# Casting reloaded weights some units after their load, and moving four small loads to another queue

## The chip, the cores and the metric

The kernel runs on one core of a Trainium2 chip. The metric is the device time of one execution in microseconds (us), from runs of the same program with the same inputs. The core has a matrix engine (PE, whose weight loads PEld are listed apart), a vector engine (DVE), a scalar engine (ACT), a third elementwise engine (POOL) and a synchronisation engine (SP) that here only issues DMA transfers. Each engine works through its own instructions in a fixed order and waits on semaphores for the results of the others. An engine that issues DMAs does so in that same order, so a waiting instruction also holds back the DMAs behind it.

## The reference

An attention with random features is followed by a gated MLP:

```python
def phi(x):                                   # x: q or k, scaled by D**-0.25
    proj = einsum('bhsd,md->bhsm', x, omega)
    h = proj - sum(x * x, -1, keepdims=True) / 2
    return exp(h - max(h, -1, keepdims=True)) / sqrt(m)
kv  = einsum('bhsm,bhsd->bhmd', k_p, v);  z = sum(k_p, 2)
out = einsum('bhsm,bhmd->bhsd', q_p, kv) / (einsum('bhsm,bhm->bhs', q_p, z) + 1e-6)

x = out.transpose(0, 2, 1, 3).reshape(4608, 512)
g = x @ w_gate;  y = (g / (1 + exp(-g)) * (x @ w_val)) @ w_out
```

Batch and heads are 8 and 8, the sequence is 576, the head size 64, and there are 128 random features. The MLP has 4608 tokens, a model width of 512 and an inner width of 1536. All inputs are 32-bit floats.

## The kernel before

**Attention** goes in steps. A step n holds one group of k and one of q of two heads, and is cut into pieces: `st_transpose` (PE, and the copy `x` on ACT at L408), `st_project` (PE `pp`, L423), `st_max` (DVE, L437 to L447), `st_exp` (ACT `ph`, L459, eight exponentials), `k_accumulate` (PE `kvacc`, L561, with v as its other operand), `q_transpose` (PE `ptq`, ACT `qt`), `q_mult` (PE `po`, L602), `q_norm` (DVE `xn`, L612) and `q_out` (PE `xt`, ACT `xo` L657, a store to DRAM). When a head's k groups are all in, `kvacc` is copied by ACT (`kvr`, L475), and PE transposes its last column (`zp`, L481). `kvacc` has a single PSUM buffer. A sequence of 576 is one group of 512 rows and a rest of 64; the rest's v is the tile `vrest`, loaded at L365, the other v tiles at L358.

**The MLP** runs between the attention's pieces, as soon as tokens are there. A 32-bit product is made of three passes of PE over a high part and a low part of each operand: `whi*xh`, `whi*xl`, `wlo*xh` (`mm1`, L678, for gate g and value v; `mm2`, L687, for the output product o). It goes by nine tiles of 512 tokens. The inner width is cut into 12 blocks, three to a weight set, so four sets. Tiles 0 to 4 visit the four sets in 20 visits; at six places the next visit needs another set, and the new weights take the place of the old in SBUF. Tiles 5 to 8 are done in pairs at the end by a scheme of seven products (L912). A visit is a sequence of units that a generator `stream()` yields: three g units, three v units, four o units, each 12 or 9 matmuls. `give()` draws units from it between the attention's pieces, so a unit is the clock of the MLP.

**Weights.** `convert_all` reads the raw weights once (the tile `st`), rounds them on ACT (L277, L289), DVE (L280 to L286) and POOL (L291) into a tile `wc`, and stores that to a DRAM scratch `wscr` (L295). When a set is changed, `load_weights` fetches a block back from the scratch (`wraw`, L323), and `split_piece` makes the two parts: ACT casts `whi` (L251) and POOL subtracts `wlo` (L252). `wc` and `wraw` share three buffers under the tag `wraw`, so a fetch waits until an earlier tile has been split, and a conversion waits for the same buffers. Reloads of gate blocks (i = 0) are asked for behind the silu of the last visit with the old set, those of value blocks (i = 1) behind each v unit, and those of output blocks (i = 2) behind the last o unit: nine blocks at each of six changes, 54 in all.

**Order.** A scheduler decides at build time, from simulated times and the order of the code, in which order each engine executes. `behind_step()` tells it that an instruction stands behind the step's last exponential on ACT and the last biased operation on DVE (`step_end`); the conversion uses it, `load_weights` does not. The k and q loads (`nat`) have three buffers and are asked for three steps ahead, as are those of v.

Of the kernel before, what the change touches and what calls it, by code (L numbers as in the profile page):

```python
# [23 lines left out]
def kernel(  # L24
# [11 lines left out]
    nc = tc.nc  # L36
# [86 lines left out]
    AHEAD = 6  # L123
# [69 lines left out]
    for n in range(NN + 1):  # L193
        vi = 0
# [111 lines left out]
    def need(f, i):  # L306
        while (f, i) not in converted:
            tick()

    def load_weights(f, i):  # L310
        need(f, i)
        fetched = fetch((f,), i)
        new_weights(f, i)
        split_piece(f, i, fetched[0])

    def fetch(fs, i, spare=None):
        raws_ = []
# [60 lines left out]
    def load_v(n):  # L378
        for i, b, g, gr in slots(n, "k"):
            rest = gr is None  # L380
            ts = (vtile, vrest)[rest]
            t = ts[nv[rest] % len(ts)]
            nv[rest] += 1
            assert t not in busy, "v's tile is still needed"
            busy.append(t)
            vrows[b, g] = t
            load_group(t, v, b, gr, True, nc.scalar if n == 0 or n < AHEAD and gr is None else nc.sync)

    box = {}
    sts = {}  # L390
# [314 lines left out]
    def down(j, k_, ht, wts, next_set, tt):  # L705
        fs = sorted(ht)
        po = ps_moe(f"o{j}_{k_}_{tt}", [P, DM])
        for n, f in enumerate(fs):
            need(f, 2)
            mm2(po, ht[f], weights[f, 2] if wts is None else wts[f], tt, n == 0, n == len(fs) - 1)  # L710
        if k_ == 0:
            acc[j, tt] = accp.tile([P, DM], F32, name=f"acc{j}_{tt}", tag="acc")
            nc.scalar.copy(acc[j, tt], po)
        else:
            a_ = acc[j, tt]
            nc.vector.tensor_tensor(a_, po, a_, op=ALU.add)  # L716
        if k_ == (NPF if j in paired else NSET) - 1:
            a_ = acc.pop((j, tt))
            for o in range(0, P, RES):
                nc.sync.dma_start(rows_of(TILES[j][0] + tt * P + o), a_[o : o + RES, :])  # L720
        if next_set is not None and tt == TILES[j][1] // P - 1:
            for f in next_set:
                load_weights(f, 2)

    def stream():

        todo = []
        for vi, (j, s_, k_) in enumerate(visits):
# [14 lines left out]
            pg, ht = {}, {}  # L743
            for f in fs:
                need(f, 0)
                pg[f] = ps_moe(f"g{vi}_{f}", [P, T])[:, 0:w]
                mm1(pg[f], weights[f, 0], xs)
                yield mm1_us(w)
# [15 lines left out]
                fetch_x(nxt[0])  # L764
            for f in fs:
                need(f, 1)
                pv = ps_moe(f"v{vi}_{f}", [P, T])[:, 0:w]
                mm1(pv, weights[f, 1], xs)
                yield mm1_us(w)
                h = pg[f]  # L770
                nc.vector.tensor_tensor(h, pv, h, op=ALU.mult)  # L771
                hh = moe.tile([P, T], F32R, name=f"hh{vi}_{f}", tag="hh", bufs=FA)[:, 0:w]
                hl = moe.tile([P, T], F32R, name=f"hl{vi}_{f}", tag="hl", bufs=FA)[:, 0:w]
                nc.scalar.copy(hh, h)  # L774
                nc.gpsimd.tensor_tensor(hl, h, hh.bitcast(F32), op=ALU.subtract)  # L775
                ht[f] = hh, hl
                if new_set:
                    load_weights(nxt[1] * FA + f - fs[0], 1)
            if final:
                make_seven((0, 0), 1, fetch((0, 1), 1))  # L780
            wts = {f: weights[f, 2] for f in fs} if vi else None
            then = range(nxt[1] * FA, nxt[1] * FA + FA) if new_set else None
            todo = [(j, k_, ht, wts, then, tt) for tt in range(w // P)]
# [267 lines left out]
    def give(us):  # L1051
        debt[0] += us
        while debt[0] > 0:
            u = next(ma, None)
            if u is None:
                debt[0] = 0.0
                return False
            debt[0] -= u
            given[0] += u
        return True  # L1060
# [108 lines left out]
```

## Time and profile before

| what | value |
|---|---|
| time, three runs | 1174.39, 1174.82, 1180.82 us; median 1174.82 us |
| the profiled execution's own time | 1172.79 us |
| its span, first to last instruction | 1171.0 us, 18724 instructions |
| PE busy | 1149.5 us (98%) |
| ACT, DVE, POOL busy | 678.3 us (58%), 630.0 us (54%), 569.1 us (49%) |
| granted PE clock | 0.999 |
| attention and MLP together, then the pairs | up to about 797 us, then to the end |

Busy time of an engine counts its instructions but not the issuing of DMAs. "ACTq" and "SPq" in a timeline are the DMA issues of ACT and SP: the duration is the time that the issue keeps the engine, not the transfer's. In a timeline a row is a run of equal instructions: start, duration of the whole run, engine, line, operation, `output<-inputs`, count, and in brackets the idle time before it with what ended it. The table of waits has, for each pair of waiting and awaited line, the total, the count and the longest. In the table of windows, each engine has its busy time and, in brackets, its number of instructions.

### The profile page before, as it was taken

To read this page: it belongs to the slowest core of one execution; us is meant where nothing else is said; L and a number is where in the kernel's file an instruction comes from. 1 tells how busy PE (TensorE), PEld (TensorE's weight loads), DVE (VectorE), ACT (ScalarE), POOL (GpSimd) and SP (SyncE) were. 2 spreads that over 40 slices of the span, in tenths; PEclk is the share of its full clock that TensorE was granted. 3 is DMA by queue.
4 is the path that set the end of the run, shared out by engine and by line. 5 is a ranking of instruction groups with operands and counts; after the bars stand their busy time and mean duration, and the time that the engine had idled before them with its cause. 6 is when DMAs were issued, how large, how long until landed. Compare 5 with 4: busy or idle time off the path is not lost.

```text
span 1171.0 us, 18724 instructions
## 1 busy us (share of the span) xinstructions
PE 1149.5 (98%) x6705; PEld 951.7 (81%) x6705; DVE 630.0 (54%) x1159; ACT 678.3 (58%) x1499; POOL 569.1 (49%) x500
## 2 busy tenths in 40 slices
PE   7999999999999999999999999999999999999998
PEld 6998778888888888888888777878778888888886
DVE  5876667535466554334332552462566666456654
ACT  5898887775666665665466665334544445444441
POOL 3342353433365465554445765244655543455551
PEclk9999999999999999999999999999999999999999
DMA  7654355643454442443232212424311112211103
GB/s 168 155 147 116 108 168 164 177 127 111 127 155 131 125 118 70 120 105 82 64 80 73 60 46 81 127 81 123 93 53 47 48 53 54 72 55 54 45 19 73
DMA packets 174109, 113.52 MB, mean 97 GB/s; under 512 B 125856, under 2 KB 144320, under 8 KB 174016
## 3 DMA queue, kind: packets, MB, share of 16 engines
q1 hardware_dynamic: 172096, 111.86, 35.2%
q8 instruction: 53, 0.87, 0.3%
q10 hardware_dynamic: 1920, 0.46, 0.2%
q14 instruction: 40, 0.33, 0.1%
HBM read 87.10 MB, written 25.18 MB: 96 GB/s over the span
## 4 chain that ended last, share of the span: by engine, by line
PE 73%; DVE 5%; ACT 3%; DMA 2%; issue 2%; POOL 1%; SPq 1%; POOLq 0%; DVEq 0%; ACTq 0%
PE o L687 22%; PE g L678 11%; PE a L912 10%; PE v L678 10%; PE c L912 5%; PE pp L423 3%; PE d L912 3%; PE kvacc L561 2%; PE ptq L585 2%; PE xt L642 2%; PE pt L400 1%; DMA wraw<-wscr 1%; ACT ph L459 1%; DMA first_b<-xs 1%; POOL wlo L252 1%
## 5 line engine op out<-in xcount | busy, mean ns | idle before, releaser
L407 POOL TENSOR_TENSOR sq<-nat 128x512 f32<-128x512 f32 x72 | 75.9, 1055 | 199.3 <-DVE st L437 157.3
L716 DVE TENSOR_TENSOR acc<-o,acc 128x512 f32<-128x512 f32 x140 | 95.6, 687 | 128.6 <-PE o L687 128.2
L459 ACT ACTIVATE ph<-pp,st 128x128 f32<-128x128 f32 x576 | 157.0, 387 | 6.4 <-DVE st L447 5.7
L444 DVE TENSOR_REDUCE st<-pp 128x4 f32<-128x512 f32 x144 | 93.3, 686 | 95.7 <-PE pp L423 95.4
L252 POOL TENSOR_TENSOR wlo<-wraw,whi 128x512 fp32r<-128x512 f32 x76 | 103.1, 1366 | 64.0 <-ACT whi L251 62.4
L678 PE MATMUL g<-xh,whi 128*128 128x512 f32 x240 | 96.3, 401 | 0.9 <-DVE sl L771 0.9
L678 PE MATMUL v<-xh,whi 128*128 128x512 f32 x240 | 95.6, 398 | 0.5 <-DVE acc L716 0.5
L687 PE MATMUL o<-whi,hh 128*128 128x512 f32 x240 | 95.9, 400 | 0.0
L423 PE MATMUL pp<-omT,x 64*128 64x128 f32 x1152 | 90.9, 289 | 4.6 <-ACT x L408 4.6
L687 PE MATMUL o<-whi,hl 128*128 128x512 f32 x240 | 93.8, 391 | 0.9 <-POOL hl L775 0.9
L775 POOL TENSOR_TENSOR hl<-sl,hh 128x512 fp32r<-128x512 f32 x60 | 77.9, 1302 | 33.7 <-ACT hh L774 33.5
L678 PE MATMUL g<-xl,whi 128*128 128x512 f32 x240 | 94.0, 392 | 0.0
L678 PE MATMUL g<-xh,wlo 128*128 128x512 f32 x240 | 94.0, 392 | 0.0
L678 PE MATMUL v<-xh,wlo 128*128 128x512 f32 x240 | 93.9, 391 | 0.0
L687 PE MATMUL o<-wlo,hh 128*128 128x512 f32 x240 | 93.9, 391 | 0.0
L678 PE MATMUL v<-xl,whi 128*128 128x512 f32 x240 | 93.6, 390 | 0.0
L423 PEld LDWEIGHTS pp<-omT,x 64*128 64x128 f32 x1152 | 73.9, 189 | 21.8 <-issue 11.6
L899 POOL TENSOR_TENSOR wlo<-wspare,whi 128x512 fp32r<-128x512 f32 (+1 forms) x40 | 40.5, 1032 | 75.0 <-ACT whi L898 68.6
L771 DVE TENSOR_TENSOR sl<-v,sl 128x512 f32<-128x512 f32 x60 | 40.9, 685 | 60.8 <-PE v L678 60.8
L251 ACT CAST whi<-wraw 128x512 fp32r<-128x512 f32 x76 | 46.6, 629 | 42.1 <-PE v L678 24.4
L525 DVE TENSOR_REDUCE dj<-jk 128x4 f32<-128x512 f32 x36 | 24.6, 685 | 83.8 <-POOL jk L521 69.1
L774 ACT CAST hh<-sl 128x512 fp32r<-128x512 f32 x60 | 37.5, 626 | 51.9 <-DVE sl L771 51.7
(257 smaller groups left out, 2938.4 us busy)
## 6 DMA issues: line engine op xcount, KB each, us to landing
wraw<-wscr SPq DMA_DIRECT2D x80, 256.0 KB, 2.7
wspare<-wscr SPq DMA_DIRECT2D x40, 256.0 KB, 2.7
wscr<-wc SPq DMA_DIRECT2D x36, 256.0 KB, 2.2
out_dram<-acc SPq DMA_DIRECT2D x72, 128.0 KB, 2.3
nat<-in_k_dram SPq DMA_DIRECT2D x64, 128.0 KB, 3.1
nat<-in_q_dram SPq DMA_DIRECT2D x64, 128.0 KB, 3.1
v<-in_v_dram SPq DMA_DIRECT2D x62, 128.0 KB, 3.0
st<-in_moe_w_gate_dram SPq DMA_DIRECT2D x12, 512.0 KB, 3.9
```

What stands on the lines that cost most here:

```text
L251: nc.scalar.copy(hi, raw)
L252: nc.gpsimd.tensor_tensor(lo, raw, hi.bitcast(F32), op=ALU.subtract)
L407: nc.gpsimd.tensor_tensor(sq, nat, nat, op=ALU.mult)
L423: nc.tensor.matmul(pp[hh][:, i, c, :], x[r, i, c * P : (c + 1) * P], omT[r], start=True, stop=True)
L444: nc.vector.tensor_reduce(st[:, 1, :, :, hh], pp[hh], axis=AX.X, op=ALU.max, negate=True)
L459: step_end["s"] = nc.scalar.activation(ph[:, c, hh * M : (hh + 1) * M], pp[hh][:, i, c, :], AF.Exp, bias=st[:, 3, i, c, hh : hh + 1], scal ...
L678: nc.tensor.matmul(ps, a_[:, ws], b_[:, c, :], start=n == 0, stop=n == 3 * NC - 1)
L687: nc.tensor.matmul(ps, a_[:, ts_], b_, start=first and n == 0, stop=last and n == 2)
L716: nc.vector.tensor_tensor(a_, po, a_, op=ALU.add)
L771: nc.vector.tensor_tensor(h, pv, h, op=ALU.mult)
L775: nc.gpsimd.tensor_tensor(hl, h, hh.bitcast(F32), op=ALU.subtract)
L912: nc.tensor.matmul(ps, a_[:, w_], b_[:, c, :], start=start and c == 0 and m == 0, stop=c == CH - 1 and m == 2, skip_group_check=True,)
```

## The change

`load_weights` now only asks for the fetch and puts the block in a list `landing` with a count of 3. `land()`, called after every unit that `give()` draws, counts all entries down; an entry at 0 gets its tiles and its cast and subtraction, now inside `behind_step()`. Where a weight is about to be used (`down`, the g and v units, and the choice of output weights of a visit), `land((f, i))` brings the list up to that block at once. So the cast stands three units behind the issue of the load, and behind the exponentials of the step. The conversion's own splits of the first set stay as they were. Second, the `vrest` loads of the first steps go to SP's queue; only step 0's are on ACT's.

```diff
--- before.py
+++ after.py
@@ -307,11 +307,22 @@
         while (f, i) not in converted:
             tick()
 
+    LAND = 3
+    landing = []
+
     def load_weights(f, i):
         need(f, i)
-        fetched = fetch((f,), i)
-        new_weights(f, i)
-        split_piece(f, i, fetched[0])
+        landing.append([LAND, f, i, fetch((f,), i)[0]])
+
+    def land(upto=None):
+
+        for t in landing:
+            t[0] -= upto is None
+        while landing and (landing[0][0] <= 0 or upto in [(f, i) for _, f, i, _ in landing]):
+            _, f, i, raw = landing.pop(0)
+            new_weights(f, i)
+            with behind_step():
+                split_piece(f, i, raw)
 
     def fetch(fs, i, spare=None):
         raws_ = []
@@ -384,7 +395,7 @@
             assert t not in busy, "v's tile is still needed"
             busy.append(t)
             vrows[b, g] = t
-            load_group(t, v, b, gr, True, nc.scalar if n == 0 or n < AHEAD and gr is None else nc.sync)
+            load_group(t, v, b, gr, True, nc.scalar if n == 0 else nc.sync)
 
     box = {}
     sts = {}
@@ -707,6 +718,7 @@
         po = ps_moe(f"o{j}_{k_}_{tt}", [P, DM])
         for n, f in enumerate(fs):
             need(f, 2)
+            land((f, 2))
             mm2(po, ht[f], weights[f, 2] if wts is None else wts[f], tt, n == 0, n == len(fs) - 1)
         if k_ == 0:
             acc[j, tt] = accp.tile([P, DM], F32, name=f"acc{j}_{tt}", tag="acc")
@@ -743,6 +755,7 @@
             pg, ht = {}, {}
             for f in fs:
                 need(f, 0)
+                land((f, 0))
                 pg[f] = ps_moe(f"g{vi}_{f}", [P, T])[:, 0:w]
                 mm1(pg[f], weights[f, 0], xs)
                 yield mm1_us(w)
@@ -764,6 +777,7 @@
                 fetch_x(nxt[0])
             for f in fs:
                 need(f, 1)
+                land((f, 1))
                 pv = ps_moe(f"v{vi}_{f}", [P, T])[:, 0:w]
                 mm1(pv, weights[f, 1], xs)
                 yield mm1_us(w)
@@ -778,6 +792,8 @@
                     load_weights(nxt[1] * FA + f - fs[0], 1)
             if final:
                 make_seven((0, 0), 1, fetch((0, 1), 1))
+            for f in fs if vi else ():
+                land((f, 2))
             wts = {f: weights[f, 2] for f in fs} if vi else None
             then = range(nxt[1] * FA, nxt[1] * FA + FA) if new_set else None
             todo = [(j, k_, ht, wts, then, tt) for tt in range(w // P)]
@@ -1055,6 +1071,7 @@
             if u is None:
                 debt[0] = 0.0
                 return False
+            land()
             debt[0] -= u
             given[0] += u
         return True
```

Behind the change the lines of the kernel are 11 to 14 higher: L365 is L376, L323 is L334, L408 is L419, L459 is L470, L475 is L486, L657 is L668, L752 is L765, L774 is L788, L775 is L789; L251 to L295 keep theirs.

The first place is the start of the program, on ACT and SP. ACT before (`om` is the matrix of random features, `x` the first scaled k and q):

```order
L334 DMA om_128<-in_omega_dram 128x64 x2
L358 DMA v_97<-in_v_dram 128x4x64
L358 DMA v_98<-in_v_dram 128x4x64
L365 DMA vrest_105<-in_v_dram 64x2x64 x4
L337 ACT_TABLE_LOAD
L337 ACTIVATE omT<-pt_om 128x128
L408 COPY x_150<-pt_145 128x512
```

and ACT in the changed kernel:

```order
L345 DMA om_128<-in_omega_dram 128x64 x2
L369 DMA v_97<-in_v_dram 128x4x64
L369 DMA v_98<-in_v_dram 128x4x64
L348 ACT_TABLE_LOAD
L348 ACTIVATE omT<-pt_om 128x128
L419 COPY x_150<-pt_145 128x512
```

The four `vrest` loads, which stood between the last v load and the load of the activation table, are gone from ACT. On SP at the same place, before (`nat` is k and q, the number behind a name tells tiles apart, `st_0` is a raw gate weight):

```order
L358 DMA v_100<-in_v_dram 128x4x64
L358 DMA v_101<-in_v_dram 128x4x64
L358 DMA v_102<-in_v_dram 128x4x64
L358 DMA v_103<-in_v_dram 128x4x64
L358 DMA nat_155<-in_k_dram 128x4x64 x2
L358 DMA v_104<-in_v_dram 128x4x64
L233 DMA st_0_343<-in_moe_w_gate_dram 128x4x256
L358 DMA nat_195<-in_k_dram 128x4x64 x2
L233 DMA st_0_459<-in_moe_w_gate_dram 128x4x256
L358 DMA nat_238<-in_k_dram 128x4x64 x2
```

and SP in the changed kernel:

```order
L369 DMA v_100<-in_v_dram 128x4x64
L376 DMA vrest_105<-in_v_dram 64x2x64 x4
L369 DMA nat_155<-in_k_dram 128x4x64 x2
L369 DMA v_101<-in_v_dram 128x4x64
L369 DMA v_102<-in_v_dram 128x4x64
L369 DMA v_103<-in_v_dram 128x4x64
L369 DMA nat_195<-in_k_dram 128x4x64 x2
L369 DMA v_104<-in_v_dram 128x4x64
L233 DMA st_0_343<-in_moe_w_gate_dram 128x4x256
L369 DMA nat_238<-in_k_dram 128x4x64 x2
```

The `vrest` loads now stand ahead of `nat_155`, the k of step 3 (counted from 0); `nat_195`, that of step 4, stands ahead of the raw weight `st_0_343` instead of behind it, `nat_238` behind it still, and the second raw weight, `st_0_459`, has gone further down.

The second place is ACT at the first change of set, from the last rows that the old set's visit has there to the copy of `kvacc` (`whi_0` and `whi_1` are casts of reloaded gate and value weights, `wc` and `st` belong to the conversion, `hh` and `sl` are the MLP's hidden values, the rest is the attention's). Before:

```order
L774 CAST hh_1_3078<-sl_1_2955 128x512
L251 CAST whi_1_3084<-wraw_1_3082 128x512
L289 ACTIVATE st_1_2903<-st_1_2903 128x512
L251 CAST whi_1_3121<-wraw_1_3119 128x512
L277 ACTIVATE wc_2_3140<-st_2_2990 128x512
L774 CAST hh_2_3115<-sl_2_2957 128x512
L752 ACT_TABLE_LOAD
L752 ACTIVATE sl_3_3253<-g_3_3125 128x512
L657 COPY xo_0_3_3150<-xt_0_3147 128x256
L587 COPY qt_2_3168<-ptq_2_3163 128x512
L475 COPY kvr_0_3174<-kvacc_0_2620 128x260
L408 COPY x_3207<-pt_3202 128x512
```

and in the changed kernel:

```order
L251 CAST whi_0_3085<-wraw_0_2961 128x512
L251 CAST whi_0_3089<-wraw_0_2963 128x512
L277 ACTIVATE wc_1_2980<-st_1_2903 128x512
L289 ACTIVATE st_1_2903<-st_1_2903 128x512
L788 CAST hh_2_3107<-sl_2_2957 128x512
L251 CAST whi_1_3126<-wraw_1_3043 128x512
L668 COPY xo_0_3_3142<-xt_0_3139 128x256
L765 ACT_TABLE_LOAD
L765 ACTIVATE sl_3_3253<-g_3_3113 128x512
L598 COPY qt_2_3160<-ptq_2_3155 128x512
L277 ACTIVATE wc_2_3132<-st_2_2978 128x512
L486 COPY kvr_0_3166<-kvacc_0_2620 128x260
```

The row ahead of this piece is the first `whi_0`, and ahead of that stands `hh_1`. The three `whi_0` casts came here from ahead of the exponentials `ph_35`, 13 rows before `hh_1` and more; the first `whi_1` cast, also from there, now stands ahead of `xo_0`, the table load, the silu `sl_3` of the new set's first g block and `kvr_0`; the other two `whi_1` went behind the next exponentials; and the conversion of `wc_2`, which was ahead of `hh_2`, stands right ahead of `kvr_0`.

The third place is POOL, from there to the output blocks that follow (`hl` is the low part of the hidden values, `sq` a square of the attention, `wlo_2` the low part of an output block). Before:

```order
L775 TENSOR_TENSOR hl_1_3079<-sl_1_2955,hh_1_3078 128x512
L252 TENSOR_TENSOR wlo_1_3085<-wraw_1_3082,whi_1_3084 128x512
L291 TENSOR_TENSOR wc_1_2992<-st_1_2903 128x512
L252 TENSOR_TENSOR wlo_1_3122<-wraw_1_3119,whi_1_3121 128x512
L775 TENSOR_TENSOR hl_2_3116<-sl_2_2957,hh_2_3115 128x512
L407 TENSOR_TENSOR sq_3494<-nat_3143 128x512
L291 TENSOR_TENSOR wc_2_3140<-st_2_2990 128x512
L407 TENSOR_TENSOR sq_3633<-nat_3289 128x512
L252 TENSOR_TENSOR wlo_2_3373<-wraw_2_3370,whi_2_3372 128x512
L252 TENSOR_TENSOR wlo_2_3379<-wraw_2_3376,whi_2_3378 128x512
L291 TENSOR_TENSOR wc_0_3273<-st_0_3138 128x512
L775 TENSOR_TENSOR hl_3_3420<-sl_3_3253,hh_3_3419 128x512
```

and in the changed kernel:

```order
L789 TENSOR_TENSOR hl_2_3108<-sl_2_2957,hh_2_3107 128x512
L291 TENSOR_TENSOR wc_1_2980<-st_1_2903 128x512
L252 TENSOR_TENSOR wlo_1_3127<-wraw_1_3043,whi_1_3126 128x512
L418 TENSOR_TENSOR sq_3494<-nat_3135 128x512
L252 TENSOR_TENSOR wlo_1_3218<-wraw_1_3066,whi_1_3217 128x512
L252 TENSOR_TENSOR wlo_1_3237<-wraw_1_3111,whi_1_3236 128x512
L291 TENSOR_TENSOR wc_2_3132<-st_2_2978 128x512
L418 TENSOR_TENSOR sq_3633<-nat_3289 128x512
L291 TENSOR_TENSOR wc_0_3273<-st_0_3130 128x512
L252 TENSOR_TENSOR wlo_2_3425<-wraw_2_3370,whi_2_3424 128x512
L252 TENSOR_TENSOR wlo_2_3429<-wraw_2_3372,whi_2_3428 128x512
L789 TENSOR_TENSOR hl_3_3408<-sl_3_3253,hh_3_3407 128x512
```

The three `wlo_0` subtractions, which stood ahead of `hl_0`, now stand between `hl_1` and the first row shown here; `wc_1` stands ahead of all `wlo_1`, and at the output blocks `wc_0` moved from behind the first two `wlo_2` to ahead of them.

PE's order is the same as before but for three matmuls of the second g block of the new set, which now stand ahead of `zp_0` and the `kvacc` that follows it. The fetches of this change stand on SP in the same turn, with one step's q and k loads now ahead of the first value block.

## The prediction

> **What bounds the kernel now.** I read the page's busy times first, then the windows by stage, then PE's waits, and only then the timelines of the places that the change touches.
>
> ```profile
> span 1171.0 us, 18724 instructions
> PE 1149.5 (98%) x6705; PEld 951.7 (81%) x6705; DVE 630.0 (54%) x1159; ACT 678.3 (58%) x1499; POOL 569.1 (49%) x500
> ```
>
> PE is busy for 98% of the span, and PE's instructions are the same after the change. So the end can move only by PE's idle time, 1171.0 - 1149.5 = 21.5 us, or by new idle time. The windows (the first PE pair of each row is its busy time) say where it lies:
>
> ```profile
> 0.00:30.00 30.00, 21.76 (x213) 19.42 (x213) 14.81 (x31) 17.67 (x56) 10.07 (x27) 1.00 0.71 167
> ...
> 212.00:330.00 118.00, 116.82 (x721) 98.40 (x719) 54.99 (x110) 79.77 (x174) 46.04 (x39) 1.00 0.50 138
> 330.00:750.00 420.00, 419.62 (x2514) 339.08 (x2513) 182.79 (x365) 247.47 (x544) 234.88 (x205) 1.00 0.34 91
> ```
>
> The first 30 us hold 8.2 us of it; the stretch with the first two changes of set, 212 to 330, 1.2 us; the next 420 us, with most of the later reloads, 0.4 us. So the casts can win almost nothing there, and can lose. PE's waits for ACT and DVE, with totals, counts and longest:
>
> ```profile
> PE pp L423 <- ACT x L408: 4.6, 4, 3.5
> PE xt L635 <- DVE xn L612: 1.1, 1, 1.1
> ```
>
> The largest is the wait of the first `pp` for ACT, and the `vrest` part of the change bears on it.
>
> **The start: four loads leave ACT.** ACT, then PE:
>
> ```profile
> 1.66 1.54 ACTq L358 DMA_DIRECT2D v<-in_v_dram  x2
> 3.30 3.40 ACTq L365 DMA_DIRECT2D vrest<-in_v_dram  x4
> 6.73 1.28 ACT L337 ACT_TABLE_LOAD   x1 [6.73 <-DMA vrest<-in_v_dram]
> 8.03 0.28 ACT L337 ACTIVATE omT<-pt_om 128x128 f32<-128x128 f32 x1
> 8.20 0.58 ACT L408 COPY x<-pt 128x512 f32<-128x512 f32 x1
> ...
> 3.91 0.45 PE L336 MATMUL pt_om<-ident,om 128*128 128x128 f32 x1 [3.91 <-DMA om<-in_omega_dram]
> 4.15 1.13 PE L400 MATMUL pt<-ident,nat 128*128 128x128 f32 x4
> 8.83 2.08 PE L423 MATMUL pp<-omT,x 64*128 64x128 f32 x16 [3.55 <-ACT x L408]
> ...
> 20.05 0.72 PE L400 MATMUL pt<-ident,nat 128*128 128x128 f32 x4
> ```
>
> Four issues keep ACT until 6.70; the table load, `omT` and `x` follow, and PE starts `pp` at 8.83 (3.55 idle), though `pt` had been done at 4.15 + 1.13 = 5.28. Without them ACT is free at 1.66 + 1.54 = 3.20: the table load ends near 4.5, `omT` (its input is there at 4.36) near 4.8, `x` can start at 5.35 and ends at 5.93, and `pp` starts near 5.98, 2.85 us earlier. That is the upper bound, unless the next, shorter wait for `x` shrinks too.
>
> What is late next is the k loads, since the four `vrest` stand on SP ahead of those of steps 3 to 5. SP's issues, with the times from issue to landing of the `nat` loads of 12.21, 14.98 and 17.08 in the three last rows:
>
> ```profile
> 3.79 4.17 SPq L365 DMA_DIRECT2D nat<-in_k_dram  x4
> 8.66 3.41 SPq L358 DMA_DIRECT2D v<-in_v_dram  x5
> 12.21 1.29 SPq L358 DMA_DIRECT2D nat<-in_k_dram  x2
> 14.23 0.64 SPq L233 DMA_DIRECT2D st<-in_moe_w_gate_dram  x1
> 14.98 1.30 SPq L358 DMA_DIRECT2D nat<-in_k_dram  x2
> 17.08 2.21 SPq L358 DMA_DIRECT2D nat<-in_k_dram  x2
> ...
> 24.54 2.61 SPq L365 DMA_DIRECT2D nat<-in_k_dram  x4
> ...
> DMA to landing us min/median/max: 2.8/2.8/2.8
> ...
> DMA to landing us min/median/max: 4.9/4.9/4.9
> ...
> DMA to landing us min/median/max: 5.3/5.3/5.3
> ```
>
> Four small issues cost 2.61 us at 24.54 but 4.17 at 3.79, beside ACT's own issues, so SP may win up to 1.56 at 3.79 and pays 2.6 for `vrest`. The k of step 4 was issued at 14.98 behind a raw weight of 512 KB and took 4.9; now its place is one raw weight earlier in the queue and one `v` and the four `vrest` later: 8.66 + 2 v (1.36) + 2.6 + 1.3 + 3 v (2.05) = 15.97, or 14.4 with the 1.56 won. With 2.8 to landing it is there at 17.2 to 18.8, and PE used it at 20.05, so 1.25 to 2.85 us of the gain stand. The k of step 5 then comes 1.3 + 0.68 + 0.64 later, 17.0 to 18.6, behind one raw weight instead of two: with 2.8 to 5.3 to landing it is there between 19.8 and 23.9. PE used it at 23.30, so this alone leaves all of the gain or takes 0.6 more than it. Bounds of the start: a loss of 0.6 and a gain of 2.85. I take a gain of **1.9**, nearer the upper end, because only one raw weight is ahead of that load and SP is freed of ACT's parallel issues.
>
> [...]
>
> **The first change of set: casts behind the exponentials.** Before:
>
> ```profile
> 228.39 2.17 ACT L459 ACTIVATE ph<-pp,st 128x128 f32<-128x128 f32 x8
> 231.57 0.62 ACT L774 CAST hh<-sl 128x512 fp32r<-128x512 f32 x1 [1.00 <-DVE sl L771]
> ...
> 233.11 0.40 PE L678 MATMUL g<-xh,wlo 128*128 128x512 f32 x1
> 239.03 0.27 PE L481 MATMUL zp<-ident,kvr 128*4 128x128 f32 x1
> ...
> 238.56 0.41 ACT L475 COPY kvr<-kvacc 128x260 f32<-128x260 f32 x1
> ...
> L252 POOL TENSOR_TENSOR wlo<-wraw,whi 128x512 fp32r<-128x512 f32 x76 | 103.1, 1366 | 64.0 <-ACT whi L251 62.4
> L775 POOL TENSOR_TENSOR hl<-sl,hh 128x512 fp32r<-128x512 f32 x60 | 77.9, 1302 | 33.7 <-ACT hh L774 33.5
> ...
> wraw<-wscr SPq DMA_DIRECT2D x80, 256.0 KB, 2.7
> wscr<-wc SPq DMA_DIRECT2D x36, 256.0 KB, 2.2
> ```
>
> First, the gate weights. `hh_1` need not wait for DVE's conversion work any more (that moves behind it), so ACT does it at the end of the exponentials, 230.56, to 231.15, and the three casts follow. POOL does `hl_1` (1.30) and then the first `wlo_0` (1.30), which ends near 233.8. PE's third matmul of the new set needs it at 233.11: a stall of **0.7 us**, bounds 0, if `hl_1` is done that much sooner, and 1.7, if `hh_1` starts at 231.57 as before.
>
> Second, the value weights. The fetch of the first `wraw_1` takes a buffer that the second `wlo_0` frees, near 235.1; landing 2.7 later, it is there near 237.9. Its cast stands on ACT ahead of `xo_0`, the table load, `sl_3`, `qt_2`, `wc_2` and `kvr_0`, so all of them stand still until then. `wc_2` waits besides for the store of `wc_1`: POOL finishes the other two `wlo_0`, `hl_2` and `wc_1` near 238.8, and with 2.2 for the store that is 241.0, plus 0.7 for `wc_2` and 0.41 for `kvr_0`: 242.1. PE wants `kvr_0` for `zp` at 239.03 + 0.7 + three matmuls of 0.23 that now stand ahead = 240.4. The stall is **1.7 us**. Its lower bound is 0 (238.6 + 0.41 is soon enough if ACT and the store are early by that much); its upper bound is the wait for landing added to it, 1.7 + 2.7 = 4.4.
>
> Third, the output weights. POOL, ACT and PE in turn:
>
> ```profile
> 259.55 2.52 POOL L252 TENSOR_TENSOR wlo<-wraw,whi 128x512 fp32r<-128x512 f32 x2 [3.49 <-ACT whi L251]
> 262.04 1.03 POOL L291 TENSOR_TENSOR wc<-st 128x512 int32<-128x512 int32 x1
> 262.11 0.68 ACT L277 ACTIVATE wc<-st 128x512 f32<-128x512 f32 x1 [1.55 <-POOL wlo L252]
> 265.43 0.41 PE L635 MATMUL xt<-ident,xn 128*128 128x128 f32 x2 [1.05 <-DVE xn L612]
> ```
>
> ACT's conversion of the next block waits for a buffer that the second `wlo_2` frees; DVE's steps of it stand ahead of `xn`, for which PE already waited 1.05 us. Now POOL's `wc` of 1.03 us stands ahead of both `wlo_2`, so the chain is **1.0 us** longer. Bounds: the wait may vanish (a gain of 1.05) if the casts that now stand behind L289 still find POOL free earlier, or double (a loss of 2.1).
>
> **The other five changes.** The same edit there meets a PE that was idle for 0.4 us in 420, and the reloads have the whole set's visits of slack behind them; ACT does wait there for landings already without PE noticing:
>
> ```profile
> 323.23 0.62 ACT L251 CAST whi<-wraw 128x512 fp32r<-128x512 f32 x1 [2.60 <-DMA wraw<-wscr]
> ```
>
> I take 0 (bounds: a gain of 0.4, PE's idle there; a loss of 2.3 at each of three changes, rival three). The cover is the MLP units already queued on PE; were it gone, the price is that of the first change's value weights. From the third conversion's end on no `wc` competes. `land()` itself adds no instruction.
>
> **Sum.** -1.9 + 0.7 + 1.7 + 1.0 = +1.5 us on the profiled execution's 1172.79 (span 1171.0), so 1174.3; the median of the runs was 1174.82, 2.0 higher, so the same sum gives **1176.3**.
>
> **Rivals.** (1) The casts cost PE nothing, because POOL and ACT are early by the 0.7 and 1.7 us that decide, and only the start remains: 1174.82 - 1.9 = 1172.9, and with the upper bound there 1172.0. For it speaks that both stalls are small sums over long chains that a scheduler has aligned; against it, that the orders put a cast that waits for a landing ahead of what PE waits for.
> (2) SP, not ACT, bounds the start, and its 2.6 us of added issues eat the gain: 1176.3 + 1.9 = 1178.2. For it: the solid rows of SP; against it: the raw weights that moved behind.
> (3) Slower: the value weight's cast stands on ACT before its fetch has landed not at one change but at the three after it as well, with the silu and the exponentials behind it. It decides where the wait for the landing is longer than the PE work queued ahead, one g unit of 12 matmuls of 0.23, 2.7 us. Three times 0.7 + 1.7 is 7.2: 1183.5. For it: 2.7 us of landing is just that; against it, 330 to 750 has 0.4 us of idle PE and nothing that must be soon.
> (4) Faster by more than 0.5%: it would take 5.9 us, and the waits that the change could reach are 4.6 for `x` and 1.05 for `xn`, 5.65 in all. Nothing else is idle enough.
>
> **Numbers.** Chances: the forecast 0.48, rival one 0.27, two 0.09, three 0.12, four 0.04. A measurement tells about 0.5%, 5.9 us, from no change: faster means below 1168.9, slower above 1180.7. The forecast, one and two lie inside but for the forecast's tail: its terms' upper bounds (1.7, 4.4 and 2.1, with none of the start's gain) would sum to 1183. So 0.05 faster, 0.82 same, 0.13 slower. The likeliest's own range is 1173 to 1180; the range of 8 in 10 reaches to rival one with its upper bound and a gain of 1.05 at the output weights (1171) and into rival three: 1171 to 1182.
>
> **What would show it.** Right: the table load on ACT near 3.2, the first `pp` near 6.0, and step 5's `pt` less than 2.85 earlier than 23.3; a PE wait of the g unit for `wlo` and one of `zp` for `kvr` near 240; a longer wait of `xt` for `xn`. Wrong: no new PE wait between 230 and 270, which makes it rival one; idle PE on L400 waiting for `nat` in the first 60 us, rival two; waits of PE on silu, `hh` or `ph` at later changes, rival three.

## The result and the profile after

The changed kernel took **1187.75 us** in the median of five runs (1184.84 to 1189.42), the kernel before 1174.82 in the same five rounds. The ratio is **1.0097**, with a 95% interval of 1.0080 to 1.0115: slower by 1% (the two medians alone give 1.0110). The forecast was 1176.3, the range 1171 to 1182; the time lies outside the range, on the side that had a chance of 0.13.

The page of the profiled execution of after, and its windows by the same stretches as before:

```profile
span 1183.5 us, 18701 instructions
PE 1156.1 (98%) x6705; PEld 956.9 (81%) x6705; DVE 630.8 (53%) x1159; ACT 678.1 (57%) x1499; POOL 569.2 (48%) x500
...
0.00:30.00 30.00, 24.26 (x216) 21.69 (x217) 15.78 (x32) 17.64 (x55) 10.09 (x27) 1.00 0.67 153
...
212.00:330.00 118.00, 114.18 (x709) 95.88 (x708) 54.42 (x110) 75.98 (x164) 42.05 (x36) 1.00 0.48 137
330.00:750.00 420.00, 415.27 (x2464) 335.73 (x2463) 182.31 (x364) 245.79 (x546) 231.50 (x202) 0.99 0.33 89
```

The span grew by 12.5 us. Two things stand out against before. PE's idle time in 330 to 750, 0.4 us before, is now 4.7. And PE's *busy* time grew by 6.6 us with the same 6705 matmuls: the granted clock of that stretch is 0.99 instead of 1.00, and at the start full clock came at 14.8 us instead of 12.5. PE's waits in after:

```profile
PE pt L411 <- ACT xo L668: 4.0, 2, 2.6
...
PE zp L492 <- ACT kvr L486: 3.1, 2, 2.5
PE pp L434 <- ACT x L419: 3.1, 4, 0.9
PE xt L646 <- DVE xn L623: 1.4, 2, 0.9
...
PE g L689 <- POOL wlo L252: 0.4, 1, 0.4
```

`pt` for `xo` and `zp` for `kvr` are new; `pp` for `x` has lost its 3.5 us at the start. Since PE's order is all but the same in both kernels, each PE instruction of after can be set beside the same one of before. The table shows by how much it starts later, from span start to span start, and so where the 12.5 us were picked up:

| place in after (us) | what happens | us |
|---|---|---|
| 0 to 46 | start: first `pp` 2.2 earlier, then given back and more | +1.6 |
| 235 | `g` waits for `wlo` of the first change | +0.65 |
| 244 | `zp` waits for `kvr`, first change | +2.2 |
| 270 | `xt` waits for `xn`, output weights of the first change | 0 |
| 342 to 357 | 0.3 won, then `pt` waits for `xo`, second change | +2.4 |
| 357 to 363 | PE at half clock | +2.65 |
| 492 to 495 | `pt` waits for `xo`, `zp` for `kvr`, third change | +2.0 |
| 496 to 500 | PE at half clock | +1.6 |
| 500 to the end | seven-product part begins with less waiting | -0.7 |

The two places that the prediction had at nothing, with the half clock behind each, are 8.65 of the 12.5 (2.4 + 2.65 + 2.0 + 1.6).

**The first change** went as the prediction's chain says, step by step. ACT, then PE:

```profile
231.96 0.67 ACT L788 CAST hh<-sl 128x512 fp32r<-128x512 f32 x1
232.47 1.72 ACT L251 CAST whi<-wraw 128x512 fp32r<-128x512 f32 x3
...
239.00 0.62 ACT L251 CAST whi<-wraw 128x512 fp32r<-128x512 f32 x1 [1.99 <-DMA wraw<-wscr]
243.22 0.66 ACT L277 ACTIVATE wc<-st 128x512 f32<-128x512 f32 x1 [0.93 <-DMA wscr<-wc]
243.78 0.36 ACT L486 COPY kvr<-kvacc 128x260 f32<-128x260 f32 x1
...
235.29 0.50 PE L689 MATMUL g<-xh,wlo 128*128 128x512 f32 x1 [0.44 <-POOL wlo L252]
244.20 0.27 PE L492 MATMUL zp<-ident,kvr 128*4 128x128 f32 x1 [2.47 <-ACT kvr L486]
```

The value weight's cast waits for its landing, the conversion behind it for the store of the one before, and `kvr` stands behind both. The wait that ended last is the one for the store. The table load, `sl`, `qt` and `xo` fill the time between.

**The second change** is the new one. In before, the conversion, `xo` and `pt` stood there without a wait:

```profile
344.22 0.66 ACT L277 ACTIVATE wc<-st 128x512 f32<-128x512 f32 x1
348.45 0.36 ACT L657 COPY xo<-xt 128x256 f32<-128x256 f32 x1
350.44 0.61 PE L400 MATMUL pt<-ident,nat 128*128 128x128 f32 x4
```

ACT, POOL and PE in after:

```profile
348.82 0.62 ACT L251 CAST whi<-wraw 128x512 fp32r<-128x512 f32 x1
353.83 0.68 ACT L277 ACTIVATE wc<-st 128x512 f32<-128x512 f32 x1 [4.39 <-POOL wlo L252]
354.54 1.28 ACT L765 ACT_TABLE_LOAD   x1
355.83 1.08 ACT L765 ACTIVATE sl<-g 128x512 f32<-128x512 f32 x2
356.80 0.38 ACT L668 COPY xo<-xt 128x256 f32<-128x256 f32 x1
...
350.05 1.29 POOL L532 TENSOR_TENSOR jk<-ph,zt 128x512 f32<-128x512 f32 x1
351.30 1.28 POOL L789 TENSOR_TENSOR hl<-sl,hh 128x512 fp32r<-128x512 f32 x1
352.53 1.27 POOL L252 TENSOR_TENSOR wlo<-wraw,whi 128x512 fp32r<-128x512 f32 x1
...
357.23 1.12 PE L411 MATMUL pt<-ident,nat 128*128 128x128 f32 x4 [2.60 <-ACT xo L668]
358.00 0.78 PE L689 MATMUL g<-xh,whi 128*128 128x512 f32 x1
358.57 0.63 PE L689 MATMUL g<-xl,whi 128*128 128x512 f32 x1
...
363.12 0.40 PE L698 MATMUL o<-whi,hh 128*128 128x512 f32 x1
```

The conversion `wc` at 353.83 needs a buffer that it shares with the reloaded weights, and gets it when POOL has done the `wlo` of the second value block, which stands behind `jk` and `hl` and ends at 353.80. ACT does nothing for 4.39 us in front of it, with the table load, two silus and `xo` behind it. `xt` and `pt` share one PSUM buffer, so PE's `pt` waits for `xo`: 2.60 us. From there to 363.1 the matmuls of 512 columns start 0.43 us apart instead of 0.23: half clock, by the clock's records from 356.1 to 362.9.

**The third change** has the same end by another way. In before, the cast of `xh` and `xo` had no wait in front of them there:

```profile
478.99 0.62 ACT L702 CAST xh<-xraw 128x512 fp32r<-128x512 f32 x1
481.97 0.43 ACT L657 COPY xo<-xt 128x192 f32<-128x192 f32 x2
```

ACT and PE in after:

```profile
491.08 0.63 ACT L713 CAST xh<-xraw 128x512 fp32r<-128x512 f32 x1 [2.49 <-DMA xraw<-xs]
491.73 1.28 ACT L765 ACT_TABLE_LOAD   x1
493.52 0.43 ACT L668 COPY xo<-xt 128x192 f32<-128x192 f32 x2
...
494.00 0.66 PE L411 MATMUL pt<-ident,nat 128*128 128x128 f32 x4 [1.40 <-ACT xo L668]
495.28 0.27 PE L492 MATMUL zp<-ident,kvr 128*4 128x128 f32 x1 [0.63 <-ACT kvr L486]
```

`xraw`, a new tile's x, has the third use of the shared buffers; the load of the third `xraw` is issued at 487.95, when a `wlo` that ends at 487.92 frees one (in before at 468.94), and its cast waits for the landing in front of the same copies.

### The profile page after: what moved, and what is told of

Read it like the earlier page. It is cut to its first block, busy times and chain, and to the rows that moved or that the text cites. A ratio compares the mean times of both kernels' runs of the same rounds, so it can differ in the third digit from the quotient of the medians.

```text
span 1183.5 us, 18701 instructions
## 1 busy us (share of the span) xinstructions
PE 1156.1 (98%) x6705; PEld 956.9 (81%) x6705; DVE 630.8 (53%) x1159; ACT 678.1 (57%) x1499; POOL 569.2 (48%) x500
## 4 chain that ended last, share of the span: by engine, by line
PE 71%; DVE 6%; ACT 3%; DMA 2%; issue 2%; POOL 2%; SPq 1%; POOLq 0%; DVEq 0%; ACTq 0%
PE o L698 22%; PE g L689 11%; PE a L928 10%; PE v L689 9%; PE c L928 5%; PE pp L434 3%; PE d L928 3%; PE kvacc L572 2%; PE ptq L596 2%; PE xt L653 2%; PE pt L411 1%; POOL wlo L252 1%; DMA first_b<-xs 1%; ACT ph L470 1%; PE po L613 0%
## 5 line engine op out<-in xcount | busy, mean ns | idle before, releaser
L470 ACT ACTIVATE ph<-pp,st 128x128 f32<-128x128 f32 x576 | 157.6, 388 | 7.2 <-DVE st L458 6.4
L789 POOL TENSOR_TENSOR hl<-sl,hh 128x512 fp32r<-128x512 f32 x60 | 78.3, 1310 | 41.7 <-ACT hh L788 41.5
L434 PEld LDWEIGHTS pp<-omT,x 64*128 64x128 f32 x1152 | 74.7, 191 | 20.3 <-issue 12.6
L788 ACT CAST hh<-sl 128x512 fp32r<-128x512 f32 x60 | 37.7, 629 | 55.8 <-DVE sl L785 55.8
L572 PE MATMUL kvacc<-v,ph 128*128 128x65 f32 x512 | 66.7, 270 | 0.0
```

Of the source, the lines that this page charges most:

```text
L434: nc.tensor.matmul(pp[hh][:, i, c, :], x[r, i, c * P : (c + 1) * P], omT[r], start=True, stop=True)
L470: step_end["s"] = nc.scalar.activation(ph[:, c, hh * M : (hh + 1) * M], pp[hh][:, i, c, :], AF.Exp, bias=st[:, 3, i, c, hh : hh + 1], scal ...
L572: nc.tensor.matmul(acc[:, 2 * (pr % 2) + hh, :], ph[:, c, hh * M : (hh + 1) * M], vt[:, 2 * c + j if gr is None else c, hh, :], start=firs ...
```

## The experiments

The theory after the two traces, **L**: the casts' delay holds the three shared buffers longer, so that other users of them (the conversion, the new tile's x) come late on ACT, in front of copies that PE waits for; the half clock behind the idle time doubled the price in this trace (4.25 us lost to it behind 4.4 us of idle time at the second and third change). The rivals: the ordering behind the exponentials alone does it; the casts themselves are late for PE; the two parts of the change only hurt together. For the start there were two theories, S and K, told below. Ratios are to the kernel before on the same chip.

**The two parts apart.** `v_only` is the kernel before with one line:

```diff
-            load_group(t, v, b, gr, True, nc.scalar if n == 0 or n < AHEAD and gr is None else nc.sync)
+            load_group(t, v, b, gr, True, nc.scalar if n == 0 else nc.sync)
```

> The kernel before with the second part of the change alone: the four left-over v loads of the first steps on SP instead of ACT. Reading of the two traces (theory S): the first pp starts 2.1 us earlier, but the slow clock of the first 15 us lasts 2.4 us longer and three waits of pp and xt between 28 and 46 us (k and q loads late on SP) take back another 1.9, so the end comes 1.7 us later than before: about +1.7 us, with 1.2 to 2.2. The prediction's reckoning: -1.9 us. If the k loads are not delayed by SP but by something in the other part of the change, -0.3 us.

`land_only` is the changed kernel with that line as before.

> The changed kernel with the v loads as before: the first part of the change alone. Theory L (the casts' delay makes the shared buffers free late, ACT waits in front of what PE needs, and two of the stalls halve PE's clock): about +11 us on before, with stalls of zp near 240 us, of pt near 357 and 494 us, and half a clock for 3.4 to 10 us in all. If the two parts of the change only cost together (a start that is later by 1.7 us shifts the rest), at most +3 us.

Measured: `v_only` 0.9994 (0.9979 to 1.0008), `land_only` 1.0125 (1.0092 to 1.0158). The whole loss is the casts' part; the v part costs nothing that can be measured. On 1175.4 the interval of `v_only` is -2.5 to +0.9 us: it holds the prediction's -1.9 and leaves out the +1.7 that one trace had suggested. That the parts only hurt together is out.

**Delay or order.** `step_only` keeps the ordering and drops the delay:

```diff
         fetched = fetch((f,), i)
         new_weights(f, i)
-        split_piece(f, i, fetched[0])
+        with behind_step():
+            split_piece(f, i, fetched[0])
```

> The kernel before with cast and subtraction of a reloaded block ordered behind the step's exponentials, but asked for at once with the load, not three units later. Theory L-delay (the three units are the cause): within 2 us of before, no stall of pt at 357 or 494. Rival L-order (standing behind the exponentials is the cause): +8 us or more, with the same stalls as the changed kernel.

`land_free` keeps the delay and drops the ordering:

```diff
             new_weights(f, i)
-            with behind_step():
-                split_piece(f, i, raw)
+            split_piece(f, i, raw)
```

> The first part of the change alone, with the casts three units behind their loads but not ordered behind the step's exponentials. If the delay of three units is enough by itself: +8 us or more on before. If only the two together hurt (the ordering alone cost nothing measurable): within 3 us of before.

`land_1` and `land_2` are `land_only` with `LAND = 1` and `LAND = 2`.

> The first part of the change alone with a delay of one unit instead of three, still behind the exponentials. If the loss comes from buffers that come free later, it shrinks with the delay: a third to a half of the 14 us, +4 to +7 us. If it is a matter of one order or the other, either about 0 or the whole +14 us.

> The first part of the change alone with a delay of two units. Theory L: what counts is whether the delay carries the casts past the end of a step, so that they are ordered behind the next step's exponentials; with one unit it did not (no change), with three it did (+14 us). Two units: part of the blocks pass, +3 to +10 us, with one or two of the three stalls. Rival (the loss needs the exact order of three): within 2 us of before.

| kernel | delay, units | behind the exponentials | ratio | 95% interval | buffer held, first change | second change |
|---|---|---|---|---|---|---|
| before | 0 | no | 1 | | 8.7 us | 8.4 us |
| step_only | 0 | yes | 1.0006 | 0.9988 to 1.0024 | 9.1 | 9.2 |
| land_1 | 1 | yes | 0.9998 | 0.9978 to 1.0018 | 9.1 | 9.2 |
| land_free | 3 | no | 1.0023 | 1.0002 to 1.0044 | 9.2 | 9.3 |
| land_2 | 2 | yes | 1.0096 | 1.0081 to 1.0111 | 12.3 | 12.7 |
| land_only | 3 | yes | 1.0125 | 1.0092 to 1.0158 | 13.4 | 12.6 |

The last two columns are worked out from each trace: from the issue of the n-th fetch to the end of the n-th subtraction, mean of the nine blocks of a change. Neither half of the edit does the harm alone. Without the order, the scheduler brings the delayed casts back to where they were; without the delay (or with one unit of it) the exponentials that they stand behind are already early enough. Two units carry the call past the next step's exponentials, so that the casts go one step further down: in the order of ACT at the first change, `land_1` still has all `whi_0` ahead of `ph_35` and all `whi_1` ahead of `ph_36`, as `step_only` and `land_free` do, while `land_2` and `land_only` have the `whi_0` behind `ph_35` and one or two `whi_1` behind `ph_36`. The buffer is then held 4 us longer, and the loss is there, all but complete. The expectation for `land_1`, a third to a half of the loss, was wrong: it is a step, not a slope. That of `land_free`, +8 us or more if the delay is enough by itself, is refuted too (+2.7 us, at the edge of what can be told).

**Whose wait it is.** `land_own` gives the conversion's tile a buffer of its own; `own_ctl` is the same edit on the kernel before.

```diff
-            u = moe.tile([P, DM], F32, name=f"wc{f}_{i}", tag="wraw", bufs=3)
+            u = att.tile([P, DM], F32, name=f"wc{f}_{i}", tag="wc", bufs=1)
...
-                    xo = att.tile(list(src.shape), F32, name=f"xo{b}_{g}_{j}", tag="xo", bufs=3)
+                    xo = att.tile(list(src.shape), F32, name=f"xo{b}_{g}_{j}", tag="xo", bufs=2)
```

> The first part of the change alone, but the conversion's tile wc has a buffer of its own and no longer shares the three buffers of the reloaded weights; to make room the tile xo has two buffers instead of three. Theory L-shared (ACT stands still in the conversion of the next block, whose buffer a late subtraction frees, with silu, xo and kvr behind it): the stalls of zp near 240 and of pt near 357 us are gone, the one near 494 (x of a new tile shares the buffers too) may stay: at most +5 us on its control. Rival L-cast (the late cast or subtraction itself is what PE or ACT waits for): +10 us or more as without the edit.

> Control of the run above: the kernel before with wc in a buffer of its own and two buffers for xo. Every theory expects it within 3 us of before; what it differs by is taken off the run above.

Measured: 1.0074 (1.0046 to 1.0102) and 1.0042 (1.0023 to 1.0060). The control is not neutral (+4.9 us: on ACT the conversions wait 26.8 us in all for stores of `wc`, where before has no such wait, and `xo` 6.0 instead of 1.1 us for its own stores), but the casts' part on top of it is now 0.0032, some 3.8 us, instead of 14.7; the two intervals overlap, so this rest is hardly told from nothing. The window of `land_own` that holds the second change:

```profile
340.00:366.00 26.00, 25.95 (x169) 20.76 (x169) 18.14 (x34) 18.01 (x38) 18.18 (x16) 1.00 0.51 150
```

PE is idle for 0.05 us of 26: the stall of the second change is gone with the shared buffer, with delay and ordering as in `land_only`. That agrees with theory L. It is not a clean cut, since the fetches no longer wait for conversions either and are issued earlier (near 268 us instead of 320 at this change); that the casts themselves are not what PE waits for is shown by the trace of after, where ACT, not PE, waits for the `wlo`, and for its buffer. At the first change a stall of `pt` stays, 1.47 us, ahead of which ACT's cast of a value weight waits 2.72 us for its landing; the control has one of 1.81 us there, behind a conversion that waits 1.60 us for a store. So the pair says nothing on the first change. At the third change a stall much like that of after stays (1.1 and 0.6 us), as L has it for the x tile, whose buffers are still shared. A wait of PE of 3.8 us that ends at 731.9, followed by half a clock (granted clock of this run 0.997, of before 0.999), comes from the edit's other half: ACT's `xo` stands still there for 5.43 us for the store of an earlier `xo`, in the control for 2.01, since `xo` has only two buffers in both. Set beside the control PE instruction by PE instruction, this run loses nothing at the second change and about 1 us at the third. That the x tile's buffer makes the third stall is read from the trace alone; no run gives it one of its own.

**Each change its own.** `land_late` delays by one unit at the first two changes, by three at the other four:

```diff
+        asked[0] += 1
-        landing.append([LAND, f, i, fetch((f,), i)[0]])
+        landing.append([LAND if asked[0] > 18 else 1, f, i, fetch((f,), i)[0]])
```

> The first part of the change alone, with a delay of one unit at the first two changes of set and of three at the other four. Theory L (each stall belongs to the delayed blocks of its own change): the stalls near 240 and 357 us are gone, the one near 490, where the cast of a new tile's x waits for its load, stays: +2 to +6 us. Rival (the third stall follows from the shift that the first two make): within 1.5 us of before.

Measured: 1.0018 (1.0001 to 1.0036), +2.1 us. PE's waits of this run between 480 and 492 us:

```profile
PE pt L413 <- ACT xo L670: 1.4, 1, 1.4
PE zp L494 <- ACT kvr L488: 0.6, 1, 0.6
```

The third stall is there alone, at the size that it has in after (1.40 and 0.63). In this run no half clock followed (granted clock 0.999, in `land_only` 0.995). The rest, 14.7 - 2.1 = 12.6 us, is therefore what the first two changes cost together with the half clock that followed the third in `land_only`; the two differences are from different chips.

**The start.** Theory S was that SP's added issues make the k and q loads late. `v_pool` issues the left-over v of the first steps from POOL and leaves SP's order as it was:

```diff
-            load_group(t, v, b, gr, True, nc.scalar if n == 0 or n < AHEAD and gr is None else nc.sync)
+            load_group(t, v, b, gr, True, nc.scalar if n == 0 else nc.gpsimd if n < AHEAD and gr is None else nc.sync)
```

> The kernel before with the four left-over v loads of the first steps issued by POOL, which is idle there, instead of ACT; SP's order is that of before. Theory S (SP's added issues made the k and q loads late): ACT is free at 3.2 as in the change, the waits of pp at 32 and 46 us are gone, and the end is 0 to 2.9 us earlier than before, about -1.0 us if the slow clock of the start lasts as long as in the changed kernel. If SP is not the cause, the same +1.7 us as in the changed kernel.

Measured: 0.9975 (0.9958 to 0.9992), -2.9 us: the best of all, and the one that is faster than before beyond its interval. Its trace doesn't show this at the start: the `pp` that starts 44 us into before starts 1.6 us later here, and the 2.15 us that make up for it are won between 763 and 778 us, where the seven-product part begins. `warm_b` is `v_pool` with transposes that are meant only to keep PE busy; the author's guess, theory C, was that full clock then comes sooner:

```diff
+    def warm(n):
+        pw = ps_moe(f"warm{n}", [P, M])
+        for _ in range(n):
+            nc.tensor.transpose(pw, ident, ident)
...
         if n == 0:
+            warm(9)
             setup_omega()
...
     st_transpose(0)
+    warm(4)
```

> The kernel before with the four left-over v loads issued by POOL, and 13 transposes of the identity more on PE, whose output nothing reads: 9 ahead of the first real one, in the 3.9 us that PE waits for omega, and 4 while it waits for the first x. [...] Rival (PE is held by ACT and the k loads there anyway): same as without, 0.9975.

Measured: 1.0012 (0.9997 to 1.0028), so nothing gained. Its trace shows the rival: full clock came earlier, the `pp` at 10.51 took 1.16 us, and then PE stood still for the next k load and lost the clock again. It is not a clean trial of theory C, since the scheduler moved SP's order too: the k of step 3 is issued at 11.87 us, behind one more v and a raw weight, in `v_pool` at 10.49, and it is this load that PE waits for at 17.15. PE, and two windows:

```profile
7.06 2.08 PE L428 MATMUL pp<-omT,x 64*128 64x128 f32 x16
10.51 1.16 PE L428 MATMUL pp<-omT,x 64*128 64x128 f32 x16 [0.68 <-ACT x L413]
17.15 0.86 PE L405 MATMUL pt<-ident,nat 128*128 128x128 f32 x4 [2.18 <-DMA nat<-in_k_dram]
...
16.00:20.00 4.00, 2.84 (x26) 2.57 (x28) 1.31 (x4) 1.90 (x7) 1.04 (x1) 0.95 1.11 260
20.00:24.00 4.00, 4.00 (x28) 3.72 (x26) 2.71 (x5) 1.35 (x4) 2.17 (x3) 0.63 0.72 161
```

`v_only` has the same picture (full clock near 10.5 us, a wait for k at 19.7, half clock behind it):

```profile
19.73 0.83 PE L400 MATMUL pt<-ident,nat 128*128 128x128 f32 x4 [1.73 <-DMA nat<-in_k_dram]
...
20.00:24.00 4.00, 4.00 (x24) 3.76 (x24) 0.69 (x1) 1.27 (x4) 1.95 (x2) 0.58 0.87 201
```

So theory K: whoever frees ACT early meets the k loads next. `k_first` puts all v loads of steps 1 to 4 on POOL and the first raw weight behind the k of step 5; `k_first_warm` adds the transposes to it.

```diff
-            load_group(t, v, b, gr, True, nc.scalar if n == 0 else nc.gpsimd if n < AHEAD and gr is None else nc.sync)
+            load_group(t, v, b, gr, True, nc.scalar if n == 0 else nc.gpsimd if n < 5 else nc.sync)
...
         if n == FIRST_RAW:
-            load_raw(0)
+            with tc.issue_after(nat_in[5].ins):
+                load_raw(0)
```

> The kernel before with the v loads of steps 1 to 4, the left-over ones too, issued by POOL, those of step 0 by ACT, and the first raw weight ordered behind the k loads of step 5 on SP, so that SP has only k loads until then. Theory K (once ACT is free early, PE waits at the start for the k loads, which stand on SP behind v and raw weights): no wait of pt for nat in the first 30 us, and the 2 to 3 us that ACT gives are kept as far as the slow clock lets them: 1170 to 1173, ratio 0.994 to 0.998. Rival (k loads are not what holds it): same as with the left-over v alone on POOL, 0.9975, or, if POOL's issues hold back its squares, slower.

> The same with the 13 unread transposes of the identity at the start. [...] If the transposes gave nothing because they delay the first pp themselves (7.1 instead of 6.6 us), the same as the run without them or 0.5 us later.

Measured: 0.9995 (0.9979 to 1.0012) and 0.9996 (0.9981 to 1.0012). In `k_first` only 0.7 us of waiting for k is left, all of it ahead of the first `x`, and still nothing is gained; both runs reached full clock only at 14.5 and 14.6 us, without the transposes and with them, so these two runs don't show theory C, and `pp` now waits for `x` again:

```profile
6.99 2.08 PE L426 MATMUL pp<-omT,x 64*128 64x128 f32 x16 [0.68 <-ACT x L411]
10.79 2.08 PE L426 MATMUL pp<-omT,x 64*128 64x128 f32 x16 [0.68 <-ACT x L411]
22.43 1.16 PE L426 MATMUL pp<-omT,x 64*128 64x128 f32 x16 [0.52 <-ACT x L411]
```

Theory K is not enough either. What is left is scatter: in these traces PE runs at half speed for the first 9 to 22 us (16 matmuls of `pp` take 2.08 us there and 1.16 behind it), and the moment of the change differs from run to run. By the clock's records it came at 12.5, 16.3, 12.1, 12.4, 16.9, 16.1 and 21.8 us in the traces of before, `step_only`, `land_1`, `land_free`, `land_only`, `land_2` and `land_late`, whose first 40 us are one program. Set by PE instructions, the `pp` that starts 44 us into the profile of before starts 1.3 to 4.6 us later in the other six of these, and 0.4 to 3.6 us later in the six runs that freed ACT. The profiled run of before was the luckiest start of its kind, and comparing one trace with it misled theory S. Whether the 2 to 3 us at the start can be had for good stays open: `v_pool` measured as much over the whole run, on one chip; `v_only`, `warm_b`, `k_first` and `k_first_warm` did not.

## Why the prediction was wrong

- **The start, a gain of 1.9 us.** The mechanism was right: the first `pp` came 2.2 us earlier in after (6.62 against 8.83), SP issued the four small k loads in 2.60 instead of 4.17 us, and the k loads were late next (0.5 us of waits for `nat`). What `v_only` measured is a gain of 0.7 us with an interval of -0.9 to 2.5, so the term is within its bounds and isn't settled. What the term did not contain is the half clock of the start, though the rows that it quotes show it (four matmuls of `pt` take 1.13 us at 4.15 and 0.72 at 20.05): in after, the 2.2 us won at the first `pp` had shrunk to 0.2 by 14.7 us, when full clock came.
- **The gate weights, 0.7 us.** Right: 0.65.
- **The value weights, 1.7 us.** Right in its chain; the stall was 2.47 us, net 2.2 with the three matmuls that moved ahead. Without the start's 1.6 us, `kvr` was done 0.5 us later than reckoned and PE was there 0.2 us earlier. The late link was POOL's `wc_1`, done 0.7 us later than reckoned: DVE's step ahead of it, L283, took 1.39 us at 236.81, beside a `wlo` on POOL, where it had taken 0.42 before.
- **The output weights, 1.0 us.** Wrong, 0: `xt` waited 0.89 us for `xn` in after, 1.05 before. The chain did get longer as reckoned: against the PE instructions around it, ACT's conversion and DVE's first step of it came 1.2 us later. DVE's next step, L283, which stands ahead of `xn`, took that back. Before, then after:

```profile
263.39 1.55 DVE L283 TENSOR_SCALAR wc<-wc 128x512 int32<-128x512 int32 x1
```

```profile
268.85 0.43 DVE L283 TENSOR_SCALAR wc<-wc 128x512 int32<-128x512 int32 x1
```
- **The other five changes, 0.** This is the step that failed. It argued that PE had been idle for 0.4 us in 420 and that the reloads had slack. The slack of the *weights* was real: PE never waited for a `wlo` or `whi` there in the trace of after. But the buffers that they hold have other users, and these stand on ACT in front of silu, `xo` and `kvr`. The trace of after and `land_own` speak for this at the second change, `land_late` shows that the third stall is its own. The first change's chain already had the conversion in it; the same term was not carried on to the second, although conversions still ran there. Idle 0.4 us in 420 says that nothing was missing, not how much was spare. "From the third conversion's end on no `wc` competes" was true (the last `wc` on ACT is at 430 us) and hid that `xraw` takes its place. What the runs showed instead of 0 is 8.65 us at the second and third change in the trace of after.
- **The rivals.** The third had the place (the later changes) and two thirds of the growth, 1183.5, but not the mechanism: it was not a weight's cast in front of its own landing. It had a chance of 0.12, and the upper bound of the range, 1182, was drawn inside it.
- **The price of an idle microsecond.** Every term was a stall and nothing else, since the prediction held at its start that the end can move only by PE's idle time, old or new; but PE's busy time grew too, from 1149.5 to 1156.1 us. In the profiled run 4.4 us of idle time at the second and third change cost another 4.25 us of half clock behind them. Together with the stalls themselves that is the 8.65 us that the sum lacked.

## What to carry to other kernels

Before delaying the last reader of a buffer, list all who take buffers of that tag, and the engine on which each of them waits in order; the slack that counts is theirs, not the data's. A delay in units and an order behind a step, each alone within 0.3% here, can together carry work over a step's end: the loss then comes as a step (0 at one unit, the whole at two). Where one engine is busy for 98%, price a new idle gap with the clock behind it (here 4.25 us behind 4.4), and don't take a start of a few microseconds from a single trace.

## What the runs showed of the hardware

Of two gaps on PE of 2 to 3 us in mid-run, one had half a clock with it and one had not. In the trace of after the gap of 2.47 us at 244 left the clock at 1.00, and with the one of 2.60 us at 357 it was 0.50; in `land_only`, with the same gaps (2.5 and 2.6 us), it was the other way about. The windows of the two kernels at the two places, after first (the first number behind the engines' pairs is the granted clock):

```profile
244.00:248.00 4.00, 3.80 (x22) 3.30 (x23) 1.64 (x3) 3.97 (x12) 0.24 (x1) 1.00 0.95 286
358.00:362.00 4.00, 4.00 (x12) 3.13 (x11) 0.21 (x1) 3.58 (x9) 1.60 (x2) 0.50 0.59 131
```

```profile
246.00:248.00 2.00, 2.00 (x8) 1.81 (x8) 0.73 (x2) 1.99 (x8) 0.00 (x0) 0.50 1.07 336
358.00:362.00 4.00, 2.06 (x11) 1.81 (x12) 2.85 (x7) 3.71 (x7) 1.42 (x1) 1.00 0.15 33
```

The half-clock stretches of after in mid-run lasted 6.83 us (356.11 to 362.94) and 3.41 us (496.06 to 499.47); the one of `land_only` comes to 3.4 us, worked out from granted clocks of 0.90, 0.50 and 0.75 in the windows 244 to 246, 246 to 248 and 248 to 250. How long PE stood still doesn't decide alone, by these traces: when the clock of after fell at 356.11, PE had been idle for 1.48 us, while the whole 2.47 us at 244 left it at 1.00. Shorter gaps had half clock behind them too: 1.73 us (`v_only`, at 19.7, with 0.58 and 0.57 in the windows 20 to 24 and 24 to 28), and 1.40 with 0.63 (after, at 494).

At the start SP's issues of four small loads took 4.17 us while ACT issued four of its own, and 2.60 us in after, where ACT did not:

```profile
3.65 2.60 SPq L376 DMA_DIRECT2D nat<-in_k_dram  x4
```

Each issue took 0.59 to 0.65 us in both; in before SP paused between them, by up to 1.07 us. Beside POOL's issues, from 8.25 to 10.75 us in `v_pool`, SP's issues of larger loads took 0.65 us apiece without such pauses. Why SP pauses is not shown.

DVE's L283 took 0.41 to 0.43 us in all 25 cases of before in which POOL had no operation under way when it began, and 0.67 to 1.56 us in the 11 in which it had; in after it was 24 and 12, with 0.41 to 0.43 and 0.66 to 1.40. Where an order moves work on POOL, the time of L283 can thus come out differently, by up to 1.1 us here. The prediction's sums left that out.
